# Two decode layers on one core: unread products in TensorE's gaps, seven down chunks straight to the output rows

## The chip, the cores and the metric

The kernel runs on one core of one Trainium2 chip. The metric is the time of one execution in device microseconds (us); before the change it is 1339.48 us, the median of three runs (1339.40, 1339.48 and 1342.05).

The engines are named as the profile names them: PE (TensorE, the matrix products), PEld (its weight loads), DVE (VectorE), ACT (ScalarE), POOL (GpSimd) and SP (SyncE, which here only issues DMAs).

## The reference

Two rows (batch B = 2, one token each, width D = 448) go through attention, a gated feed-forward stage, the same attention again and the same feed-forward stage again. The same weights and the same caches are read in both rounds.

```python
def _A_ref(x, k_cache, v_cache, wq, wo):           # H = 16 heads, Dh = 256, Sk = 4096 cached keys
    q = (x @ wq) ...                                # (B, H, 1, Dh)
    scores = jnp.einsum("bhqd,bhkd->bhqk", q, k_cache) * (Dh ** -0.5)
    p = _softmax(scores, axis=-1)
    o = jnp.einsum("bhqk,bhkd->bhqd", p, v_cache)
    return o ... @ wo

def _B_ref(x, W_gate, W_up, W_down):                # F = 1792
    gate = jnp.einsum("bsd,df->bsf", x, W_gate)
    up = jnp.einsum("bsd,df->bsf", x, W_up)
    h = gate * (gate > 0) * up
    return jnp.einsum("bsf,fd->bsd", h, W_down)

x = x + _A_ref(_layernorm(x), ...)
x = x + _B_ref(_layernorm(x), ...)
x = x + _A_ref(_layernorm(x), ...)
x = x + _B_ref(_layernorm(x), ...)
```

Everything is float32. The caches are 2 x 134 MB, and each of the two attention rounds (a "pass" below) reads them once, except for some chunks that stay in the core between the passes.

## The kernel before

**Tiling.** A unit u is one pair of head and batch row; a pass has 32 units (u = 0 to 31). The 4096 keys of a unit lie 32 to a partition, so a unit's keys are four chunks of 128 x 2048 numbers (1 MB), and its values four more. All loads go into one buffer, `arena`, of 27 slots of 1 MB. `pump` (L109) issues the next load on SP as soon as a slot for it has been released in the program's order; the instruction on SP then waits until the slot's last reader is done. Chunks of keys (k), chunks of values (v), the projections of a head (h: wq and wo, 896 KB), seven loads of gate and up weights (w_in, 896 KB each) and four loads of down weights (w_out, 896 or 672 KB) all pass through it in one fixed order. The last twelve k and v chunks of a pass are loaded one by one, then come the seven w_in and the four w_out. 22 slots with k, v and h of the last units of the first pass are kept, so that the second pass, which runs the units backwards, finds them in place.

**Attention.** Every step of the loop (L443 on) mixes three units: `score` of unit u on DVE and ACT (products L344, sums L349 and L346; the kept chunks at the start of the second pass take the form L338), the softmax of u, `weigh` of unit u - 1 on PE (L385), and the end of unit u - 2: `out_add` (DVE L399), `out_turn` (PE L407), `out_keep` (DVE L416) and `project` (PE L426, every second unit). `weigh` of a chunk is four products, each of two columns of probabilities with 512 numbers a row; they go to the output rows 0, 32, 64 and 96 of one half of `po_all`, one product to each strip of 32 rows. Units 30 and 31 have no more scores behind them: the last `weigh` (unit 31, chunk 3), `out_copy` (ACT L396), `out_add`, `out_turn`, `out_keep` and `project` follow each other, and `absorb` (ACT L226, PE L228, L216, L218, DVE L236) takes the pass's result into the turned row `xs`.

**Feed-forward.** `proj` (PE L477) makes the gate from w_in 0 to 3 and, after `add_rows` (L241) and the variance (L252), the up part from w_in 3 to 6: 16 products each, four at a time in four strips. DVE L500 multiplies, PE L504 and L506 turn the result, DVE L510 and ACT L515 copy it to `hT` and `tails`, and the down products (PE L528) run over 14 chunks k of 128 hidden numbers, chunk k in strip k % 4 of `pd`. After the first pass `absorb(pd, ...)` takes `pd` up; at the end of the kernel ACT L537 copies `pd` to `row`, one product (L241) adds it to `y`, the two output rows 96 and 97 of `acc`, DVE L552 copies `y`, and SP L553 stores it.

**Start of a pass.** `first_query` (L318) makes the queries of units 0 and 1 on PE (L271, L279), copies them with ACT L325 and takes the root of the variance (ACT L253). `nsr` and `sr` are written by DVE L448 and L447 after the first chunk's score; ACT L365 is the first exponential of the pass.

The lines L119, L226 and so on are those of the profile of the kernel before.

Of the kernel before, what the change touches and what calls it, by code (L numbers as in the profile page):

```python
# [8 lines left out]
F32 = mybir.dt.float32  # L9
AF = mybir.ActivationFunctionType  # L10
# [4 lines left out]
B, D, H, S, DH, F = 2, 448, 16, 4096, 256, 1792  # L15
P = 128
DC = 5
FULL, TAIL = 3, 64
# [47 lines left out]
def two_layers(  # L66
# [10 lines left out]
    nc = tc.nc  # L77
# [16 lines left out]
    pending = []  # L94
# [14 lines left out]
    def pump():  # L109
        while pending:  # L110
            (kind, name, c), n = pending[0]
            last = at_of.get((kind, name, c - 1)) if kind in "kv" else None
            at = units.take(n, kind, last)
            if at is None:
                return
            pending.pop(0)
            src = source((kind, name, c), n)
            dst = arena[:, at * UNIT : at * UNIT + src.shape[1]]
            nc.sync.dma_start(dst, src)  # L119
            for k in range(n):  # L120
                at_of[kind, name, c + k] = at + k

# [4 lines left out]
    def release(*key):  # L127
        units.free.add(at_of.pop(key))
        pump()
# [79 lines left out]
    acc = ps_a.tile([P, D], F32, name="acc")  # L209
    nc.vector.memset(acc, 0.0)  # L210
    y = acc[SUMS : SUMS + B]

    def turned(out, rows, rhs, **flags):

# [7 lines left out]
    def absorb(rows, n, rhs, nrhs):  # L222


        sums = work.tile([P, 1], F32, name="sums")
        nc.scalar.activation(row[:n, :D], rows, AF.Copy, accum_out=sums[:n])  # L226
        minus = ps_s.tile([P, B], F32, name="small")
        nc.tensor.matmul(minus, sums[:n].to_broadcast([n, P]), nrhs[:n], start=True, stop=True)  # L228
        pt = ps_s.tile([P, DC, B], F32, name="small")
        turned(pt, row[:n], rhs[:n], start=True, stop=True)  # L230
        less = work.tile([P, B], F32, name="less")
        nc.vector.tensor_copy(less, minus)
        for part in (less[:, None, :].to_broadcast([P, DC, B]), pt):
            for p, c in spans:
                x_c = xr[p, c]
                nc.vector.tensor_add(x_c, x_c, part[p, c, :, None].to_broadcast(x_c.shape))  # L236
        nc.vector.tensor_copy(xs[:, :, 32:], xs[:, :, 31:32])

    def add_rows(n, rhs, start=False, stop=False):

        nc.tensor.matmul(y, rhs[:n], row[:n, :D], start=start, stop=stop)  # L241

    def squares():
        sq = work.tile([P, FULL + 1, B], F32, name="sq")
        nc.vector.tensor_mul(sq, xT[:, : FULL + 1], xT[:, : FULL + 1])
        total = work.tile([P, B], F32, name="total")
        nc.vector.reduce_sum(total, sq.rearrange("p c b -> p b c"), axis=AX.X)
        return total

    def deviation(total):  # L250
        var = ps_s.tile([P, B], F32, name="small")
        nc.tensor.matmul(var, ones.to_broadcast([P, P]), total, start=True, stop=True)  # L252
        nc.scalar.activation(rstd, var, AF.Sqrt, bias=eps_t, scale=1.0 / D)  # L253
# [4 lines left out]
    def attention(order, after, begun):  # L258
# [58 lines left out]

        def first_query():  # L318

            total = squares()  # L320
            pq = ps_q.tile([P, B, DH], F32, name="pq")
            w = get("h", order[0][0], 0)
            for u, at in ((0, HEAD), (1, 0)):
                query_of(u, pq)
                nc.scalar.activation(w[:, at : at + DH], q_of[u], AF.Copy)  # L325
                q_of[u] = w[:, at : at + DH]
                if u == 0:
                    deviation(total)

        def score(u, c):  # L330
            kt = get("k", order[u], c).rearrange("p (t n) -> p t n", t=CT)
# [45 lines left out]
        def weigh(u, c):  # L377


            vt = get("v", order[u], c)  # L380
            if c == 0:
                po_of[u] = po_all[:, u % 2]
            for t in range(CT // 2):
                n = c * CT + 2 * t
                nc.tensor.matmul(  # L385
                    po_of[u][32 * t : 32 * t + 2, :],
                    p_of[u][:, n : n + 2],
                    vt[:, 2 * t * DH : (2 * t + 2) * DH],
                    start=(c == 0),
                    stop=(c == NC - 1),  # L390
                )
            if ("v", order[u], c) not in after:
                release("v", order[u], c)

        def out_copy(u):
            nc.scalar.activation(row[:, :DH], po_of[u][:, :DH], AF.Copy, scale=r_of[u][:, 0:1])  # L396
# [21 lines left out]
        def project(u):  # L418
            h = order[u][0]
            if u % 2 == 0:  # L420
                return
            wo = get("h", h, 0)[:, FULL * DH + P :]
            for c in range(2):
                n = u - 1 + c
                at = 32 * (n % 3)
                nc.tensor.matmul(  # L426
                    acc[at : at + B], oT_of[h][:, c, :], wo[:, c * D : (c + 1) * D],
                    start=(n < 3), stop=(n >= n_u - 3),
                )
            if ("h", h, 0) not in after:  # L430
                release("h", h, 0)

# [32 lines left out]
    def ffn(last):  # L465


        absorb(acc[:SUMS], SUMS, lead, nlead)
        total = squares()

        def proj(parts):

            p = ps_f.tile([P, D], F32, name="pf")
            for n, (part, c, done) in enumerate(parts):
                w = get("in", "", part)
                for j in range(4):
                    nc.tensor.matmul(  # L477
                        p[32 * j : 32 * j + 32, :],
                        xs[:, c, :32],
                        w[:, j * D : (j + 1) * D],  # L480
                        start=(n == 0),
                        stop=(n == 3),
                    )
                if done:
                    release("in", "", part)
            return p

        pg = proj([(0, 0, True), (1, 1, True), (2, 2, True), (3, 3, False)])  # L490
        add_rows(SUMS, lead)
        deviation(total)
        inverse()
        scaled = work.tile([P, B], F32, name="scaled")
        nc.vector.tensor_mul(scaled, sel, rstd)
        nc.vector.tensor_mul(scaled, scaled, rstd)
        hid = row[:, :D]
        nc.scalar.activation(hid, pg, AF.Relu)
        pu = proj([(3, 4, True), (4, 0, True), (5, 1, True), (6, 2, True)])
        nc.vector.tensor_mul(hid, pu, hid)  # L500

        ph = ps_f.tile([P, 4, P], F32, name="pf")
        for m in range(FULL):
            nc.tensor.transpose(ph[:, m, :], hid[:, m * P : (m + 1) * P], ident)  # L504
        for half in (0, TAIL):
            nc.tensor.matmul(  # L506
                ph[half : half + TAIL, FULL, :], hid[:, FULL * P :], ident, start=True, stop=True
            )
        hT = row[:, : FULL * P].rearrange("p (m r) -> p m r", m=FULL)
        nc.vector.tensor_copy(hT, ph[:, :FULL])  # L510

        tails = row[:, FULL * P : FULL * P + 64].rearrange("p (m r) -> p m r", m=2)
        for k, half in enumerate((slice(0, TAIL), slice(TAIL, P))):
            pairs = ph[half, FULL, :].rearrange("p (m k r) -> p k m r", m=2, k=2)
            nc.scalar.activation(tails[half], pairs[:, k], AF.Copy)  # L515

        stat = [hT[:, m, 32 * j : 32 * j + 32] for j in range(4) for m in range(FULL)]
        stat += [tails[:, m, :] for m in range(2)]
        if not last:
            nscaled = work.tile([P, B], F32, name="nscaled")  # L520
            nc.vector.tensor_scalar_mul(nscaled, scaled, -1.0 / D)
        pd = ps_f.tile([P, D], F32, name="pf")
        for j in range(4):
            w = get("out", "", j)
            first_k = (14 * j + 2) // 4
            for k in range(first_k, (14 * j + 16) // 4):
                g4 = k % 4
                nc.tensor.matmul(  # L528
                    pd[32 * g4 : 32 * g4 + 32, :],
                    stat[k],  # L530
                    w[:, (k - first_k) * D : (k - first_k + 1) * D],
                    start=(k < 4),
                    stop=(k >= 10),
                )
            release("out", "", j)
        if last:
            nc.scalar.activation(row[:, :D], pd, AF.Copy)  # L537
            add_rows(P, scaled, stop=True)
        else:
            absorb(pd, P, scaled, nscaled)  # L540
        return scaled

# [5 lines left out]
    scaled = ffn(False)  # L548
    attention(second, set(), lambda: add_rows(P, scaled))
    ffn(True)  # L550
    found = row[SUMS : SUMS + B, :D]
    nc.vector.tensor_copy(found, y)  # L552
    nc.sync.dma_start(out.rearrange("b s d -> (b s) d"), found)  # L553


# [49 lines left out]
```

## Time and profile before

| | |
|---|---|
| median of three runs | 1339.48 us |
| the profiled execution: its own time | 1341.89 us |
| its span, first to last instruction | 1340.1 us |
| outside the span | 1.8 us |
| mean granted TensorE clock | 0.672 |
| busy: DVE, PE, ACT, PEld, POOL | 76%, 42%, 30%, 14%, 8% |
| moved by DMA | 563.22 MB, mean 420 GB/s |

Times in the profile count from the first instruction of the span. "x32" behind a group of instructions is their number; every float32 product stands as two records on PE, so 16 products are x32. In the chain of waits a line gives the start, the length and what the time went to; a DMA in it is counted from its issue to its landing. In the table by stretches, the columns are the stretch, its length, the busy time of each engine with the number of instructions, the granted PE clock (1.00 is full, 0.50 half), the busy share of the DMA engines and GB/s.

### The profile page before, as it was taken

How to read it: one execution, taken by the hardware profiler on the slowest of the kernel's cores; microseconds unless marked ns; L12 is line 12 of the kernel's file. 1: busy time of each engine (PE TensorE's matmuls, PEld its weight loads, DVE VectorE, ACT ScalarE, POOL GpSimd, SP SyncE). 2: the span in 40 equal slices, each digit the busy share in tenths (PEclk: the TensorE clock that was granted, in tenths of full speed). 3: DMA queues.
4: the chain of work that ended last, by engine and by line, in shares of the span. 5: the costliest groups of instructions: out<-in, count | busy, mean ns of one | idle time of the engine just before them, and what ended most of it. 6: DMA issues, size and time to landing. Idle time of an engine off the chain costs nothing.

```text
span 1340.1 us, 10126 instructions
## 1 busy us (share of the span) xinstructions
PE 560.5 (42%) x3046; PEld 188.2 (14%) x3046; DVE 1012.3 (76%) x1180; ACT 407.1 (30%) x1730; POOL 107.1 (8%) x192
## 2 busy tenths in 40 slices
PE   3433424434244342343574444434344342443447
PEld 2111101111011110112131111111011110111112
DVE  4997876877868768677629999988778678777781
ACT  2433333333333333330012333333333333332331
POOL 0210000000000000000001111110000000000010
PEclk9667667665666676766776666675666666766668
DMA  9999999999999999999989999999999999999997
GB/s 400 431 434 429 432 425 434 431 433 428 427 433 431 433 428 430 428 436 423 419 329 365 382 423 435 433 431 430 427 434 432 427 431 433 427 432 431 434 415 298
DMA packets 29150, 563.22 MB, mean 420 GB/s; under 512 B 3236, under 2 KB 3240, under 8 KB 10024
## 3 DMA queue, kind: packets, MB, share of 16 engines
q1 hardware_dynamic: 29092, 562.58, 98.5%
q8 instruction: 24, 0.39, 0.1%
q14 instruction: 30, 0.25, 0.0%
q10 hardware_dynamic: 4, 0.00, 0.0%
HBM read 562.56 MB, written 0.00 MB: 420 GB/s over the span
## 4 chain that ended last, share of the span: by engine, by line
DMA 59%; DVE 29%; PE 8%; ACT 2%; issue 2%; POOL 0%; DVEq 0%; SPq 0%; POOLq 0%; ACTq 0%
DMA arena<-in_k_cache_dram 56%; DVE arena L344 16%; DVE scores L349 10%; DMA arena<-in_v_cache_dram 3%; PE pq L300 2%; DVE arena L338 2%; PE acc L426 2%; PE pf L477 1%; ACT arena L346 1%; DVE row L399 1%; DMA arena<-in_w_out_dram 1%; PE pq L304 1%; PE pq L271 0%; PE small L216 0%; PE pf L528 0%
## 5 line engine op out<-in xcount | busy, mean ns | idle before, releaser
L344 DVE TENSOR_TENSOR arena<-arena 128x2048 f32<-128x2048 f32 x236 | 539.3, 2285 | 152.6 <-DMA arena<-in_k_cache_dram 147.4
L346 ACT ACTIVATE arena<-arena 128x256 f32<-128x256 f32 x708 | 286.0, 405 | 539.8 <-DVE arena L344 539.8
L349 DVE TENSOR_REDUCE scores<-arena 128x5 f32<-128x1280 f32 x236 | 350.6, 1486 | 8.2
L385 PE MATMUL po<-arena,probs 128*2 128x512 f32 x2048 | 302.9, 739 | 128.9 <-DMA arena<-in_v_cache_dram 116.5
L407 PE MATMUL small<-ones,row 128*128 128x1 f32 x256 | 61.9, 346 | 414.5 <-DVE row L399 414.5
L426 PE MATMUL acc<-arena,oT 128*2 128x448 f32 x128 | 52.8, 924 | 195.0 <-DVE oT L416 195.0
L346 ACT ACTIVATION_READ_ACCUMULATOR arena<-arena 128x1 f32 x708 | 132.4, 187 | 0.0
L407 PEld LDWEIGHTS small<-ones,row 128*128 128x128 f32 x256 | 56.4, 307 | 476.6 <-DVE row L399 476.6
L385 PEld LDWEIGHTS po<-arena,probs 128*2 128x2 f32 x2048 | 55.0, 96 | 324.7 <-issue 304.1
L357 POOL PARTITION_ALL_REDUCE top<-mx x64 | 49.4, 771 | 594.4 <-DVE mx L355 594.4
L300 PE MATMUL pq<-arena,xs 128*33 128x256 f32 x174 | 74.2, 593 | 11.7 <-DMA arena<-in_w_head_dram 11.7
L316 POOL PARTITION_BROADCAST arena<-arena x58 | 30.0, 586 | 527.6 <-ACT arena L312 500.4
L355 DVE TENSOR_REDUCE mx<-scores 128x1 f32<-128x32 f32 x64 | 11.9, 186 | 69.5 <-ACT arena L346 66.0
L362 ACT ACTIVATE nm<-top,nsr 128x1 f32<-128x1 f32 x64 | 18.8, 294 | 142.5 <-POOL top L357 142.5
L312 ACT ACTIVATE arena<-pq 33x256 f32<-33x256 f32 x29 | 10.9, 376 | 140.8 <-PE pq L304 140.8
L399 DVE SCALAR_TENSOR_TENSOR row<-po,ri,row 128x256 f32<-128x256 f32 x64 | 30.5, 477 | 17.5 <-ACT row L396 17.4
L396 ACT ACTIVATE row<-po,ri 128x256 f32<-128x256 f32 x64 | 29.6, 462 | 31.8 <-PE po L385 31.8
L300 PEld LDWEIGHTS pq<-arena,xs 128*33 128x33 f32 x174 | 25.3, 163 | 80.7 <-issue 79.1
L338 DVE SCALAR_TENSOR_TENSOR junk<-arena,pq 128x256 f32<-128x256 f32 x64 | 26.9, 420 | 8.0 <-DMA arena<-in_k_cache_dram 6.0
L369 POOL PARTITION_ALL_REDUCE total<-rs x64 | 27.0, 422 | 64.3 <-ACT probs L365 64.3
L426 PEld LDWEIGHTS acc<-arena,oT 128*2 128x2 f32 x128 | 3.0, 82 | 197.7 <-DVE oT L416 197.7
L365 ACT ACTIVATE probs<-scores,nm,sr 128x32 f32<-128x32 f32 x64 | 26.4, 413 | 2.1
(94 smaller groups left out, 260.9 us busy)
## 6 DMA issues: line engine op xcount, KB each, us to landing
arena<-in_k_cache_dram SPq DMA_DIRECT2D x57, 4096.0 KB, 44.7
arena<-in_v_cache_dram SPq DMA_DIRECT2D x57, 4096.0 KB, 52.8
arena<-in_w_head_dram SPq DMA_DIRECT2D x31, 896.0 KB, 39.4
arena<-in_v_cache_dram SPq DMA_DIRECT2D x19, 1024.0 KB, 20.5
arena<-in_k_cache_dram SPq DMA_DIRECT2D x16, 1024.0 KB, 25.6
arena<-in_w_in_dram SPq DMA_DIRECT2D x14, 896.0 KB, 18.4
arena<-in_w_out_dram SPq DMA_DIRECT2D x4, 896.0 KB, 16.8
arena<-in_w_out_dram SPq DMA_DIRECT2D x4, 672.0 KB, 9.2
```

Source lines behind the costliest of these rows:

```text
L300: nc.tensor.matmul(q, xs[:, c, :], w[:, c * DH : (c + 1) * DH], start=(c == 0), stop=False)
L316: nc.gpsimd.partition_broadcast(q_of[v], found[32 * b : 32 * b + 1], channels=P)
L338: nc.vector.scalar_tensor_tensor(junk if kept else kt[:, t, :], kt[:, t, :], 1.0, q_of[u], op0=ALU.mult, op1=ALU.mult, accum_out=found[:, ...
L344: nc.vector.tensor_mul(kt, kt, q_of[u][:, None, :].to_broadcast([P, CT, DH]))
L346: nc.scalar.activation(kt[:, t, :], kt[:, t, :], AF.Copy, accum_out=found[:, t : t + 1])
L349: nc.vector.reduce_sum(found[:, BY_ACT:], kt[:, BY_ACT:, :], axis=AX.X)
L357: nc.gpsimd.partition_all_reduce(mx_of[u], mx, P, RED.max)
L385: nc.tensor.matmul(po_of[u][32 * t : 32 * t + 2, :], p_of[u][:, n : n + 2], vt[:, 2 * t * DH : (2 * t + 2) * DH], start=(c == 0), stop=(c ...
L396: nc.scalar.activation(row[:, :DH], po_of[u][:, :DH], AF.Copy, scale=r_of[u][:, 0:1])
L399: nc.vector.scalar_tensor_tensor(row[:, :DH], po_of.pop(u)[:, DH:], r_of[u][:, 1:2], row[:, :DH], op0=ALU.mult, op1=ALU.add,)
L407: nc.tensor.matmul(pT_of[u][:, c : c + 1], row[:, c * P : (c + 1) * P], ones, start=True, stop=True,)
L426: nc.tensor.matmul(acc[at : at + B], oT_of[h][:, c, :], wo[:, c * D : (c + 1) * D], start=(n < 3), stop=(n >= n_u - 3),)
```

## The change

Six edits:

- `busy(n, half)` is new: it multiplies two columns of the identity with n x 128 columns of the identity, at most 512 in one product, into output rows 0 and 1 of one half of `po_all`. Nothing reads the result. It is called after each chunk that `weigh` does for the last two units of a pass (n = 8, two products of 512), after the last `project` (n = 5, a product of 512 and one of 128) and between `absorb` and the gate products (n = 2, one of 256).
- `first_query` ends with an exponential of `eps_t` into `nsr`, which is written again by DVE later.
- In the last feed-forward stage the first seven down chunks go to `pd` as before; then `pd` is copied and added to `y`, and the chunks 7 to 13 are multiplied straight into `y`, with two columns each: `near` and `near_tails`, the columns of `hT` and `tails` that belong to the two rows, times 1/std squared.
- The last load of the kernel (w_out 3, three chunks) is issued as two DMAs: two chunks, then one.
- `y` is copied in two halves, one by DVE and one by ACT.
- Three small DVE products make `square`, `near` and `near_tails`.

```diff
+            parts = [0, src.shape[1]]
+            if not pending:
+                parts[1:1] = [src.shape[1] - D]
+            for i, j in zip(parts, parts[1:]):
+                nc.sync.dma_start(dst[:, i:j], src[:, i:j])
...
+    def busy(n, half):
+        for k in range(0, n, 4):
+            m = min(4, n - k)
+            nc.tensor.matmul(
+                po_all[:B, half, : m * P], ident[:, :B],
+                ident[:, None, :].to_broadcast([P, m, P]), start=True, stop=True,
+            )
...
+            nc.scalar.activation(nsr[:, :1], eps_t, AF.Exp)     # end of first_query
...
+            if u >= n_u - 2:                                    # end of weigh
+                busy(8, (u + 1) % 2)
...
+            if u == n_u - 1:                                    # in project, before the release
+                busy(5, 0)
...
         absorb(acc[:SUMS], SUMS, lead, nlead)
+        busy(2, 0)
         total = squares()
...
+        n_pd = 7 if last else 14
...
+                if k < n_pd:
+                    nc.tensor.matmul(
+                        pd[32 * g4 : 32 * g4 + 32, :], stat[k], w_k,
+                        start=(k < 4), stop=(k >= n_pd - 4),
+                    )
+                else:
+                    nc.tensor.matmul(y, close[k], w_k, start=False, stop=(k == 13))
+                if last and k == n_pd - 1:
+                    nc.scalar.activation(row[:, :D], pd, AF.Copy)
+                    add_rows(P, scaled)
...
-    nc.vector.tensor_copy(found, y)
+    nc.vector.tensor_copy(found[:, : D // 2], y[:, : D // 2])
+    nc.scalar.activation(found[:, D // 2 :], y[:, D // 2 :], AF.Copy)
```

In the rows that follow, each is a line of the code, the operation, output and inputs by their names in the program, the shape of what is written, and how often it stands there in a row; the line numbers of the changed kernel differ from those of the kernel before.

**PE at the end of the second pass**, from the last `weigh` of unit 30 to the gate products. Before (`po<-arena,probs` is `weigh`, `small<-ones,row` is `out_turn`, `acc<-arena,oT` is `project`):

```order
L385 MATMUL po<-arena,probs 2x512 x16
L407 MATMUL small<-ones,row 128x1 x2
L426 MATMUL acc<-arena,oT 2x448 x2
L228 MATMUL small<-nlead,sums 128x2
L216 MATMUL small<-lead,row 128x2 x3
L218 MATMUL small<-lead,row 64x2 x2
L477 MATMUL pf<-arena,xs 32x448 x16
```

After, from the last chunk of unit 31 on (`po<-ident` is `busy`):

```order
L401 MATMUL po<-arena,probs 2x512 x4
L222 MATMUL po<-ident 2x512 x2
L425 MATMUL small<-ones,row 128x1 x2
L444 MATMUL acc<-arena,oT 2x448 x2
L222 MATMUL po<-ident 2x512
L222 MATMUL po<-ident 2x128
L242 MATMUL small<-nlead,sums 128x2
L230 MATMUL small<-lead,row 128x2 x3
L232 MATMUL small<-lead,row 64x2 x2
L222 MATMUL po<-ident 2x256
L498 MATMUL pf<-arena,xs 32x448 x16
```

The first two rows of the second list stand there eight times, once for each chunk of units 30 and 31, with the `out_turn` of unit 30 between the fourth and the fifth. The end of the first pass reads the same. So 16 products of 512 columns, and behind `project` 896 columns more, stand in PE's queue at each of the two ends.

**PE at the end of the kernel**, behind the turning of the hidden row. Before:

```order
L504 MATMUL pf<-ident,row 128x128 x3
L506 MATMUL pf<-ident,row 64x128 x2
L528 MATMUL pf<-arena,row 32x448 x14
L241 MATMUL acc<-row,scaled 2x448
L591 UNCONDITIONAL_BRANCH
```

After:

```order
L525 MATMUL pf<-ident,row 128x128 x3
L527 MATMUL pf<-ident,row 64x128 x2
L568 MATMUL pf<-arena,row 32x448 x7
L255 MATMUL acc<-row,scaled 2x448
L573 MATMUL acc<-arena,near 2x448 x5
L573 MATMUL acc<-arena,near_tails 2x448 x2
L631 UNCONDITIONAL_BRANCH
```

The product with `scaled`, which needs ACT's copy of `pd`, has moved ahead of seven of the chunks, and those seven all write the rows 96 and 97 of `acc`.

**ACT at the start of the second pass**, from the take-up of the first feed-forward result to the first exponential. Before:

```order
L226 ACTIVATE row,sums<-pf 128x448
L325 ACTIVATE arena<-pq 128x256
L253 ACTIVATE rstd<-small,eps_t 128x2
L325 ACTIVATE arena<-pq 128x256
L312 ACTIVATE arena<-pq 33x256
L362 ACTIVATE nm<-top,nsr 128x1
L365 ACT_TABLE_LOAD
L365 ACTIVATE probs,rs<-scores,nm,sr 128x32
```

After:

```order
L240 ACTIVATE row,sums<-pf 128x448
L340 ACTIVATE arena<-pq 128x256
L267 ACTIVATE rstd<-small,eps_t 128x2
L340 ACTIVATE arena<-pq 128x256
L344 ACT_TABLE_LOAD
L344 ACTIVATE nsr<-eps_t 128x1
L326 ACTIVATE arena<-pq 33x256
L378 ACTIVATE nm<-top,nsr 128x1
L381 ACTIVATE probs,rs<-scores,nm,sr 128x32
```

The table load has moved from the first softmax to `first_query`, and a write of `nsr` now stands ahead of DVE's.

More of the change, by code (lines that the diff above doesn't have):

```diff
@@ L118, in pump @@
             dst = arena[:, at * UNIT : at * UNIT + src.shape[1]]
-            nc.sync.dma_start(dst, src)
+            parts = [0, src.shape[1]]
[3 more added lines that the diff above has]
+                nc.sync.dma_start(dst[:, i:j], src[:, i:j])
             for k in range(n):
@@ L521, in ffn @@
             nc.vector.tensor_scalar_mul(nscaled, scaled, -1.0 / D)
+        else:
+            square = work.tile([P, B], F32, name="square")
+            nc.vector.tensor_mul(square, rstd, rstd)
+            near = work.tile([P, FULL, 4, B], F32, name="near")
+            nc.vector.tensor_mul(
+                near, hT.rearrange("p m (j b r) -> p m j b r", j=4, b=B)[..., 0],
+                square[:, None, None, :].to_broadcast([P, FULL, 4, B]),
+            )
+            near_tails = work.tile([P, 2, B], F32, name="near_tails")
+            nc.vector.tensor_mul(
+                near_tails, tails.rearrange("p m (b r) -> p m b r", b=B)[..., 0],
+                square[:, None, :].to_broadcast([P, 2, B]),
+            )
+            close = [near[:, m, j, :] for j in range(4) for m in range(FULL)]
+            close += [near_tails[:, m, :] for m in range(2)]
         pd = ps_f.tile([P, D], F32, name="pf")
+        n_pd = 7 if last else 14
         for j in range(4):
@@ L527, in ffn @@
                 g4 = k % 4
[L528 to L534, printed above, removed]
+                w_k = w[:, (k - first_k) * D : (k - first_k + 1) * D]
+                if k < n_pd:
+                    nc.tensor.matmul(
+                        pd[32 * g4 : 32 * g4 + 32, :], stat[k], w_k,
+                        start=(k < 4), stop=(k >= n_pd - 4),
+                    )
+                else:
+                    nc.tensor.matmul(y, close[k], w_k, start=False, stop=(k == 13))
+                if last and k == n_pd - 1:
+                    nc.scalar.activation(row[:, :D], pd, AF.Copy)
+                    add_rows(P, scaled)
             release("out", "", j)
[L536 to L539, printed above, removed]
+        if not last:
             absorb(pd, P, scaled, nscaled)
```

## The prediction

> **What bounds the kernel now.** I read the table by stretches first, for the DMA column, then the chain of waits at the two places where a pass ends, then PE's timeline there. Four stretches (columns: stretch, length, busy of PE, PEld, DVE, ACT and POOL, PE clock, DMA share, GB/s):
>
> ```profile
> 671.00:678.00 7.00, 5.87 (x32) 3.00 (x32) 1.64 (x10) 1.91 (x3) 0.00 (x0) 0.50 0.24 100
> 678.00:700.00 22.00, 16.09 (x111) 6.83 (x104) 3.38 (x16) 1.76 (x6) 0.00 (x0) 0.89 0.99 388
> 700.00:740.00 40.00, 18.52 (x95) 6.37 (x94) 38.50 (x147) 9.18 (x35) 4.90 (x6) 0.71 0.90 353
> 760.00:1329.00 569.00, 242.31 (x1334) 77.19 (x1330) 444.59 (x383) 186.85 (x807) 50.76 (x84) 0.66 1.00 429
> ```
>
> From 760 us on the DMA engines are full (429 GB/s) to the end of the stream. Between the passes they starve: 100 GB/s in 671 to 678, 353 in 700 to 740. So two things count: the middle, where all that makes the next loads late is lost for good, because the stream behind it has no slack, and the tail behind the stream. Elsewhere PE can be slow for nothing.
>
> The chain in the middle:
>
> ```profile
> 675.29 5.60 PE pf L477 x32
> ...
> 684.40 9.20 DMA arena<-in_w_out_dram
> ...
> 701.09 2.85 DVE arena L338 x16
> ```
>
> The gate products (PE, half clock) free the slots of w_in 0, 1 and 2, into which w_in 5, 6 and the first w_out are loaded; the last w_out lands at 693.60, and DVE begins the second pass at 701.09. DVE runs at 38.50 of 40 us behind that, and its scores free the slots for the next loads, so its start sets when the stream is full again.
>
> The chain at the end, and the weight load that waits for the last w_out:
>
> ```profile
> 1319.35 6.13 PE pf L477 x32
> ...
> 1326.54 3.19 PE pf L477 x32
> ...
> 1335.58 0.55 ACT row L537
> ...
> 1336.18 0.93 PE acc L241 x2
> ...
> 1337.13 0.63 DVE row L552
> ```
> ```profile
> 1334.51 0.15 PEld L528 LDWEIGHTS pf<-arena,row 128*32 128x32 f32 x6 [0.78 <-DMA arena<-in_w_out_dram]
> ```
>
> PE has its other down products done just before that load lands: at the end PE and the stream arrive together, and whatever makes PE later makes the kernel longer.
>
> **The price of an unread product.** PE rows of 703 us at full clock: one product of 448 columns, and three of 256 into the same 33 rows (then two of 128). Behind them the rows of the two ends:
>
> ```profile
> 703.04 0.92 PE L241 MATMUL acc<-row,scaled 128*2 128x448 f32 x2
> 703.89 1.48 PE L300 MATMUL pq<-arena,xs 128*33 128x256 f32 x6
> ```
> ```profile
> 1307.48 0.61 PE L407 MATMUL small<-ones,row 128*128 128x1 f32 x4 [1.11 <-DVE row L399]
> 1308.02 2.76 PE L385 MATMUL po<-arena,probs 128*2 128x512 f32 x24
> 1311.67 1.04 PE L385 MATMUL po<-arena,probs 128*2 128x512 f32 x8 [0.90 <-DMA arena<-in_v_cache_dram]
> 1313.83 0.60 PE L407 MATMUL small<-ones,row 128*128 128x1 f32 x4 [1.11 <-DVE row L399]
> 1314.68 1.35 PE L426 MATMUL acc<-arena,oT 128*2 128x448 f32 x4 [0.25 <-DVE oT L416]
> ...
> 1332.08 3.38 PE L528 MATMUL pf<-arena,row 128*32 128x448 f32 x28 [0.66 <-DVE row L510]
> ```
>
> Twelve `weigh` products in three rounds of four strips take 2.76 us, one round 1.04: a further round costs 0.86, that is 0.86 for 512 columns when four strips run side by side. The unread products all write rows 0 and 1, one strip. No row has a string of them. Bounds: 0.86 / 4 = 0.215 each if products of one strip ran side by side as those of four do, 0.99 if one after the other (three of 256, 768 columns, take 1.48). I take **0.86**, since L300's three share their rows and take nearly three times 0.43. A 448-column product in a string is 0.75 by the same rate. The Trainium skill ("TensorE: Matmul & The Clock Gate", Part 3, on packing small matmuls) says that small products run side by side when each has its own strip of the array; by it one strip gains nothing and the sum stays, while at 0.215 it would end near 1333. Rows and page agree on four strips, and no row here shows two-column products packed in one.
>
> **End of the second pass.** `busy(8)` is two products, 1.7 us at full clock; seven calls (14 products, 12.0 us) stand ahead of the last `weigh`. Queued behind them on PE are the next `weigh`, `out_turn` and `project`. What they can hide in is PE's waiting: 1.11 before `out_turn` of unit 30 and 0.90 for the last v chunk; some 0.2 of run-out between rounds goes too. 12.0 - 2.2 = **+9.8** for the last `weigh`. The v chunks have landed by then, so no DMA hides it. From there to the gate products: the eighth call +0.6 (1.7 against the gap of 1.11); `project` at full clock -0.35; 640 columns (1.07) against ACT's copy (0.7) +0.4; `absorb`'s ten records -0.9 by these rows, 2.18 us at half clock (first) and 1.28 at full (second, the middle's other absorb); 256 columns (0.43) fit the 0.41 gap. Together -0.3.
>
> ```profile
> 1316.76 0.59 PE L228 MATMUL small<-nlead,sums 96*128 96x2 f32 x2 [0.72 <-ACT row L226]
> ...
> 1318.56 0.38 PE L218 MATMUL small<-lead,row 96*64 96x2 f32 x4
> 1319.35 6.13 PE L477 MATMUL pf<-arena,xs 128*32 128x448 f32 x32 [0.41 <-issue]
> ```
> ```profile
> 695.39 0.38 PE L228 MATMUL small<-nscaled,sums 128*128 128x2 f32 x2 [0.80 <-ACT row L226]
> ...
> 696.38 0.28 PE L218 MATMUL small<-scaled,row 128*64 128x2 f32 x4
> ```
>
> What the change buys is the gate at full clock: 6.13 becomes 3.2 like the up part, **-2.9**. The clock rows that say so:
>
> ```profile
> 652.86:656.27 3.41, 2.93 (x16) 1.03 (x19) 3.19 (x17) 0.00 (x0) 0.00 (x0) 0.50 1.02 423
> 1297.97:1301.38 3.41, 2.08 (x12) 0.76 (x16) 3.38 (x5) 1.03 (x6) 0.00 (x0) 0.50 1.01 420
> 1301.38:1304.80 3.42, 3.42 (x20) 1.09 (x16) 2.06 (x3) 1.94 (x9) 0.35 (x1) 0.50 1.02 419
> 1311.62:1315.04 3.42, 2.00 (x14) 0.72 (x16) 0.64 (x2) 0.47 (x1) 0.00 (x0) 1.00 1.03 428
> 1315.04:1325.28 10.24, 9.11 (x48) 3.82 (x45) 1.64 (x10) 1.91 (x3) 0.00 (x0) 0.50 1.01 418
> ```
>
> The clock changes at edges 3.41 us apart. After a stretch with 2.93 or 3.42 us of PE work it is full, after 2.08 it stays half, after 2.00 (0.6 of it one-column products) it falls. With PE never idle it will be up from the first or second edge after 1299 and stay. The same page, Part 1, says that these windows run free of the kernel, so that the moment varies; by it the rise could come up to one window earlier or later in each pass, 1.7 us of full-clock work either way, and the middle of the sum is the same.
>
> The down stage then starts +6.6 late (9.8 - 0.3 - 2.9), at 1338.7, long after the last w_out. It took 5.68 us (1332.08 to 1337.76). Now: seven chunks in two rounds 1.7; ACT's copy of `pd` 0.65 with its hand-overs, for which PE waits with all else queued behind it; `add_rows` 0.75; seven products in one strip 7 x 0.75 = 5.25 and 0.17 to run out; half a copy 0.4 instead of 0.63. Together 8.9, **+3.3**. `near` and its kin (DVE, 0.16 us each by their like) lie beside the first rounds; the split load lands before PE asks, worth nothing. If that cover went, PE arriving early, the split would save one or two products. End: 9.8 - 0.3 - 2.9 + 3.3 = **+9.9**.
>
> **The middle.** The same 12.0 us meet more waiting:
>
> ```profile
> 660.24 0.61 PE L407 MATMUL small<-ones,row 128*128 128x1 f32 x4 [1.11 <-DVE row L399]
> ...
> 663.78 1.04 PE L385 MATMUL po<-arena,probs 128*2 128x512 f32 x8 [1.10 <-DMA arena<-in_v_cache_dram]
> 666.26 1.70 PE L385 MATMUL po<-arena,probs 128*2 128x512 f32 x8 [1.44 <-DMA arena<-in_v_cache_dram]
> 669.05 1.01 PE L407 MATMUL small<-ones,row 128*128 128x1 f32 x4 [1.09 <-DVE row L399]
> 670.32 1.66 PE L426 MATMUL acc<-arena,oT 128*2 128x448 f32 x4 [0.25 <-DVE oT L416]
> ```
>
> 12.0 - 3.65 - 0.35 of run-outs = +8.0; the last `weigh`, `out_turn` and `project` at full clock -0.65, -0.4 and -0.65; `absorb` -0.9; the eighth call and the 640 columns +0.9. The gate starts **+6.3** late, at 681.6. From there to the last w_out's landing it took 18.3 us before. Its six remaining loads (four of 896 KB, two of 672) are 5.05 MB, 13.0 us at 388 GB/s; the first is let go after one round of the gate, 0.95 instead of 1.7, and the next two follow 0.75 apart instead of 1.5, so the engines start together and hardly idle. I take 15.5, **-2.8** (bounds: the 2.4 that the gate itself gains, and 3.5).
>
> `nsr`: ACT's second query copy, the table load that moves, and DVE's write of `nsr`:
>
> ```profile
> 703.15 0.39 ACT L325 ACTIVATE arena<-pq 128x256 f32<-128x256 f32 x1 [1.94 <-PE pq L279]
> ...
> 714.09 1.28 ACT L365 ACT_TABLE_LOAD   x1
> ```
> ```profile
> 704.13 0.16 DVE L448 TENSOR_SCALAR nsr<-rstd 128x2 f32<-128x2 f32 x1
> ```
>
> The exponential ends at 703.45 + 1.28 + 0.3 = 705.03; DVE's write of the same tile has to wait for it, **+0.9**, with all scores queued behind. The load that goes at 714.09 held up nobody on DVE. At the kernel's start the same wait is hidden by a full buffer of keys. Middle: 6.3 - 2.8 + 0.9 = **+4.4**.
>
> **Sum.** +9.9 + 4.4 = +14.3 us. The profiled execution took 1341.89 (1340.1 of span and 1.8 around it), 2.4 above the median of the three runs; on the median the sum gives 1353.8, and I forecast **1353.5**.
>
> **Rivals.** (1) The products hide, and the hot clock is a gain. It turns on the price of one product in one strip: at 0.215 the 14 take 3 us, less than the middle's 3.65 of waiting; the middle gains about 4.5, the end 2 (last landing 1334.5, one product, half a copy): 1333. The point is near 0.5 us a product; against it speak L300 and L241. Chance 0.08, and 0.04 for a price near that point, which gives no change (within 0.2%, 2.7 us, about what a measurement can tell). (2) The change doesn't do what it says: two columns in one strip do not count as work for the clock. Then each product costs 1.7, the gate stays at 6, the seven down products take 10.5: some +22 and +11 at the end, +20 in the middle, about 1393. For it: no stretch of one strip's work is in the trace; against: narrow products in four strips raise the clock. Chance 0.04. (3) My forecast, 0.84, of its own between 1349 and 1358: one clock window (1.7) and a run-to-run 2.5 are its width.
>
> The range 1344 to 1360 holds the last and a little of a dearer or cheaper middle. Slower 0.88, same 0.04, faster 0.08.
>
> **What would show it.** PE busy without a gap from the first `weigh` of unit 30, 1.7 us between chunks; the last `weigh` some 8 us (middle) and 10 us (end) later, long after its chunk landed; the gate at 3.2 us and clock 1.00; seven pairs of records 0.75 apart into `acc`; DVE idle 0.9 us before `nsr`. I am wrong if unread products start closer than 0.8 us to each other at full clock, or if the last `weigh` still waits for a DMA.

## The result and the profile after

| | before | after |
|---|---|---|
| median | 1339.60 us (4 runs, 1339.40 to 1342.05) | 1362.11 us (4 runs, 1359.06 to 1363.64) |
| ratio, 95% interval | | 1.0161 [1.0139, 1.0183] |
| the profiled execution and its span | 1341.89, 1340.1 us | 1359.06, 1357.3 us |

The change makes the kernel 22.5 us slower. Slower was forecast, but with 1353.5 us and an upper end of 1360, so the time lies outside the range. The two profiled executions differ by 17.2 us only: the one of before took 2.3 us more than the median of its kernel, and the one of after is the fastest of its four, 3.1 us below the median.

Three lines of the page of the kernel after: the span, the unread products (L222) as a group, and ACT's `out_copy` (L414; it is L396 in the kernel before). In a group's line, busy time and mean length (ns) stand behind the first bar; behind the second stands the engine's idle time ahead of the group, and what ended most of it.

```profile
span 1357.3 us, 10287 instructions
...
L414 ACT ACTIVATE row<-po,ri 128x256 f32<-128x256 f32 x64 | 29.6, 462 | 52.1 <-PE po L222 38.0
...
L222 PE MATMUL po<-ident 128*2 128x512 f32 (+2 forms) x76 | 36.9, 609 | 0.0
```

The middle line matters. `out_copy` reads what `weigh` made, yet 38.0 of the 52.1 us that ACT idled ahead of it were ended by an unread product. In the page of before, all of its 31.8 us were ended by `weigh` (L385). The forecast had no such wait. The 38.0 us are not its price: most of that time ACT would have waited for `weigh` anyway.

Two stretches of the kernel after, in the columns of the table by stretches:

```profile
671.00:685.00 14.00, 12.67 (x68) 4.07 (x70) 2.29 (x12) 2.39 (x4) 0.00 (x0) 1.00 0.12 49
...
760.00:1335.00 575.00, 248.06 (x1328) 77.06 (x1324) 446.77 (x376) 187.70 (x812) 51.84 (x86) 0.67 1.00 429
```

The hole in the stream between the passes is now 14 us long at 49 GB/s (before: 7 us at 100), while PE is busy 12.67 of these 14 us, at full clock, and 7.47 of them are unread products. From 760 us on the stream is as full as before, 429 GB/s.

The chain of waits at the end of the second pass:

```profile
1325.08 0.86 PE po L401 x5
1325.94 1.29 PE po L222 x3
...
1327.65 0.86 PE po L401 x5
1328.51 1.73 PE po L222 x4
1330.24 0.02 issue
1330.27 0.48 ACT row L414
...
1335.88 3.10 PE pf L498 x32
...
1347.34 0.55 ACT row L575
...
1348.85 5.28 PE acc L573 x14
```

A chunk now comes every 2.57 us (1325.08, 1327.65): 0.86 for `weigh` and 1.71 for two unread products. Behind the last chunk PE does 1.73 us of unread products first, and only then does ACT begin its `out_copy`. The gate (L498) takes 3.10 us at full clock instead of 6.13 at half. The seven down products into `y` (L573) take 5.28 us, one after the other. No DMA is left in this chain: the last v chunk landed at 1317.4, and the last `weigh` began some 9 us later (1326.64).

The middle: the chain from the gate to the end of `first_query`.

```profile
684.24 3.10 PE pf L498 x32
...
690.88 10.14 DMA arena<-in_w_out_dram
...
709.37 1.28 ACT L344
710.67 0.21 ACT nsr L344
710.90 0.17 DVE nsr L468
```

The last w_out lands at 701.03 instead of 693.60, and DVE's write of `nsr` (L468) is now in the chain behind ACT's table load and exponential.

### The profile page after: what moved, and what is told of

Its sections match the earlier page's. It is cut to its first block, busy times and chain, and to the rows that moved or that the text cites. A ratio compares the mean times of both kernels' runs of the same rounds, so it can differ in the third digit from the quotient of the medians.

```text
span 1357.3 us, 10287 instructions
## 1 busy us (share of the span) xinstructions
PE 583.2 (43%) x3122; PEld 189.5 (14%) x3122; DVE 1012.7 (75%) x1183; ACT 407.8 (30%) x1733; POOL 106.8 (8%) x192
## 4 chain that ended last, share of the span: by engine, by line
DMA 53%; DVE 32%; PE 11%; ACT 2%; issue 2%; DVEq 0%; POOL 0%; SPq 0%; POOLq 0%; ACTq 0%
DMA arena<-in_k_cache_dram 52%; DVE arena L360 16%; DVE scores L365 11%; PE pq L314 2%; PE po L222 2%; PE acc L444 2%; DVE junk L354 2%; DVE arena L354 1%; PE po L401 1%; ACT arena L362 1%; DVE row L417 1%; PE pf L498 1%; DMA arena<-in_w_out_dram 1%; PE pq L285 1%; PE pq L318 1%
## 5 line engine op out<-in xcount | busy, mean ns | idle before, releaser
L401 PE MATMUL po<-arena,probs 128*2 128x512 f32 x2048 | 315.1, 738 | 122.3 <-DMA arena<-in_v_cache_dram 112.6
L417 DVE SCALAR_TENSOR_TENSOR row<-po,ri,row 128x256 f32<-128x256 f32 x64 | 30.5, 477 | 39.5 <-ACT row L414 39.4
L414 ACT ACTIVATE row<-po,ri 128x256 f32<-128x256 f32 x64 | 29.6, 462 | 52.1 <-PE po L222 38.0
L222 PE MATMUL po<-ident 128*2 128x512 f32 (+2 forms) x76 | 36.9, 609 | 0.0
L385 POOL PARTITION_ALL_REDUCE total<-rs x64 | 24.6, 385 | 61.7 <-ACT probs L381 61.7
```

Of the source, the lines that this page charges most:

```text
L222: nc.tensor.matmul(po_all[:B, half, : m * P], ident[:, :B], ident[:, None, :].to_broadcast([P, m, P]), start=True, stop=True,)
L401: nc.tensor.matmul(po_of[u][32 * t : 32 * t + 2, :], p_of[u][:, n : n + 2], vt[:, 2 * t * DH : (2 * t + 2) * DH], start=(c == 0), stop=(c ...
L417: nc.vector.scalar_tensor_tensor(row[:, :DH], po_of.pop(u)[:, DH:], r_of[u][:, 1:2], row[:, :DH], op0=ALU.mult, op1=ALU.add,)
```

## The experiments

Each was timed against the kernel before on the same chip, and each ratio is against that kernel. The first four ran on one chip (the kernel before took 1340.07 us there), the next four on another (1340.58), the last two on a third (1340.77), so a difference between experiments of two chips can be off by some 0.7 us for that alone. A diff is against the changed kernel where the text doesn't say otherwise, and `...` marks what is left out of it.

**The changed kernel again** (no edit).

> The changed kernel again, for a second profile. Theory A (unread products in line ahead of the last weigh, out_copy of units 30 and 31 kept waiting by the products behind its own weigh, the write of nsr, the serial down products): 1359 to 1364 us, ACT's out_copy again starting within 0.1 us of the end of a product of busy. Rival B (the time above the forecast comes from where the clock's windows happen to fall): a run nearer 1363 shows a gate or a weigh at half clock that the first profile has at full, and the same out_copy waits cost nothing.

1361.41 us (4 runs), ratio 1.0162 [1.0147, 1.0177]. This run is called the control below. The time holds. In this execution, too, all four `out_copy` at the passes' ends begin within 0.1 us of the end of an unread product. Its gate between the passes started 0.9 us earlier than in the first profile, and the copy of its first query came 1.8 us later, behind products at half clock (the windows stand in the last section). So rival B has a share in the spread between executions. It does not make the 22 us: the fastest run of the changed kernel (1359.06) is 15 us above the slowest of all runs of the kernel before (1343.71), and the changed kernel's first four runs spread over 4.6.

**The products in a tile of their own.**

```diff
+    spare = []
     def busy(n, half):
...
-                po_all[:B, half, : m * P], ident[:, :B],
+                spare[0][:B, : m * P], ident[:, :B],
...
         n_u = len(order)
+        spare[:] = [ps_f.tile([P, 4 * P], F32, name="pf")]
```

> The same products write a tile of their own in place of po_all. Theory A: out_copy of units 30 and 31 then starts within 0.1 us of its own last weigh; each of the four waits of 1.7 us turns into at most 0.6, so 4.4 us less than the control (4 x 1.1), about 1357.5. Rival C (out_copy waits because it stands behind the products in PE's order, whatever they write): no change against the control, within 1 us.

1356.71 us, ratio 1.0121 [1.0106, 1.0136]: 4.7 us less than the control, as theory A has it. ACT's timeline around the end of the first pass, the changed kernel:

```profile
666.55 0.47 ACT L414 ACTIVATE row<-po,ri 128x256 f32<-128x256 f32 x1 [7.37 <-PE po L222]
678.63 0.47 ACT L414 ACTIVATE row<-po,ri 128x256 f32<-128x256 f32 x1 [11.61 <-PE po L222]
```

and with the products in their own tile (`out_copy` is L417 there, `weigh` L404):

```profile
664.71 0.47 ACT L417 ACTIVATE row<-po,ri 128x256 f32<-128x256 f32 x1 [5.51 <-PE po L404]
675.63 0.47 ACT L417 ACTIVATE row<-po,ri 128x256 f32<-128x256 f32 x1 [10.45 <-PE po L404]
```

What comes behind it on PE, in the changed kernel and then with the products in their own tile (`out_turn` is L428 there, the products L224):

```profile
676.71 1.88 PE L222 MATMUL po<-ident 128*2 128x512 f32 x4
679.68 0.61 PE L425 MATMUL small<-ones,row 128*128 128x1 f32 x4 [1.08 <-DVE row L417]
```
```profile
675.38 1.88 PE L224 MATMUL pf<-ident 128*2 128x512 f32 x4
677.19 0.61 PE L428 MATMUL small<-ones,row 128*128 128x1 f32 x4
```

In the changed kernel PE does two products for nothing and then still waits 1.08 us for DVE; with the tile of their own `out_turn` follows the products without a gap. PE's order is the same in both; what changed is whom `out_copy` waits for. So the order of PE (rival C) is not the cause. `busy` writes the half of `po_all` that `out_copy` doesn't read; the wait goes by the tile, not by the half.

**No unread product at all** (`busy` returns at once; the other edits stay).

> The change without any unread product; the exponential into nsr, the seven direct down chunks, the split load and the two half copies stay. Theory A: before + 1.0 (nsr) + 3.5 (down stage) = about 1344. Rival D (the direct chunks cost only because PE comes late; with PE on time they save the copy and the last add): before + 1.0 - 2 = about 1338.5.

1344.77 us, ratio 1.0036 [1.0022, 1.0050]. The chain of its end:

```profile
1333.50 0.55 ACT row L570
...
1335.01 5.28 PE acc L568 x14
```

With PE on time the serial down products (L568) take the same 5.28 us, and all of it stands in the chain: rival D falls. So of the 22 us about 4.7 come from the other edits, and 16.6 (1361.4 - 1344.8) from the unread products.

**The products alone**, in the kernel before.

```diff
+    def busy(n, half):
...
             if ("v", order[u], c) not in after:
                 release("v", order[u], c)
+            if u >= n_u - 2:
+                busy(8, (u + 1) % 2)
...
+            if u == n_u - 1:
+                busy(5, 0)
...
+        busy(2, 0)
         total = squares()
```

> The kernel before with the unread products alone. Theory A: the control less 4.7 (nsr 1.0, down stage 3.7), about 1357, that is 17 to 18 us above the kernel before. Rival D: the control less 1, about 1361, since the down stage costs nothing by itself.

1355.51 us, ratio 1.0120 [1.0101, 1.0138]: 15.4 us above the kernel before, and the control less 5.9. This is nearer to A (1357) than to D, which wanted 1361. The two parts alone, 15.4 and 4.7, add up to 20.1 of the control's 21.3.

**The exponential alone**, in the kernel before.

```diff
                 if u == 0:
                     deviation(total)
+            nc.scalar.activation(nsr[:, :1], eps_t, AF.Exp)
```

> The kernel before with only the exponential into nsr at the end of first_query. Theory A: DVE's write of nsr in the second pass waits some 0.9 us for it, and the stream behind takes that over: before + 0.9. Rival F (the stream makes the wait good later, as the first pass does): within 0.3 of before.

1341.44 us (12 runs) against 1340.58, ratio 1.0006 [0.9998, 1.0015]. DVE's timeline in the second pass has the wait:

```profile
702.30 0.17 DVE L449 TENSOR_SCALAR nsr<-rstd 128x2 f32<-128x2 f32 x1 [0.86 <-ACT nsr L329]
```

The wait of 0.86 us is there; whether the total takes it over stays open, since the interval holds both 0 and 0.9 us.

**Half the products**: as in the second experiment, with `busy(4, ...)` behind each chunk.

> As the kernel with the products in a tile of their own (1356.7), with one product of 512 columns per chunk in place of two. Theory A (every product ahead of the last weigh costs its 0.86 us in line): 14 x 0.43 x 2 = 12.0 less for the two of each call, that is 6.0 less at each pass's end, 1344 to 1346. Rival G (what costs is that anything stands between the chunks, not its length): less than 4 us less, above 1352.

1344.68 us, ratio 1.0040 [1.0025, 1.0055]: 12.0 us less than the second experiment. Ahead of the last `weigh` of each pass seven products of 0.86 us have gone, 14 in all, which is 12.0 us. The products cost by their length; rival G falls.

**Products only where PE waits**, in the kernel before, in a tile of their own.

```diff
+            if u == n_u - 1:
+                busy((0, 2, 4, 5)[c])
...
+            if u == n_u - 1:
+                busy(1)
...
+            if u == n_u - 1:
+                busy(3)
...
+        busy(2)
```

The four calls stand at the end of `weigh` of unit 31 for chunk c, behind its `out_turn`, in its `project` and behind `absorb`: seven products in each pass.

> The kernel before with unread products, in a tile of their own, only where PE waits at the end of a pass: 256 columns behind chunk 1 of unit 31, 512 behind chunk 2, 640 behind chunk 3, 128 behind out_turn, 384 behind project, 256 behind absorb. Theory A: no product is in the way by more than 0.2 us, the clock stays full into the gate; the middle gains 2 to 4 us, the end nothing, since PE then waits for the last w_out: 1336 to 1338. Rival H (the middle's gain is lost again while PE waits for the last w_in, as the clock falls there): 1339 to 1340.

1336.53 us (6 runs) against 1340.58, ratio 0.9967 [0.9956, 0.9978]: faster than both kernels. PE at the end of its first pass (L396 `weigh`, L218 the products, L420 `out_turn`, L495 the gate):

```profile
666.36 1.04 PE L396 MATMUL po<-arena,probs 128*2 128x512 f32 x8 [0.60 <-DMA arena<-in_v_cache_dram]
667.22 1.24 PE L218 MATMUL pf<-ident 128*2 128x512 f32 x4
668.52 0.61 PE L420 MATMUL small<-ones,row 128*128 128x1 f32 x4
...
672.69 3.38 PE L495 MATMUL pf<-arena,xs 128*32 128x448 f32 x32
```

The last `weigh` still waits for its chunk, 0.60 us, so the products ahead of it cost nothing; `out_turn` follows them without a gap; the gate starts at 672.69 instead of 675.29 and takes 3.38 us instead of 5.60. The end of the kernel gains nothing of its own: from the last but one `project` on it takes 41.7 us in this profile and 40.8 in that of before. The gate is done at full clock there, but then PE waits 0.54 and 1.23 us for the last w_in, the clock falls, and the 14 down products take 5.60 us where they took 3.38 before. PE's row of that wait and of the down products, and the windows of the clock over them:

```profile
1320.69 0.96 PE L495 MATMUL pf<-arena,xs 128*32 128x448 f32 x8 [1.23 <-DMA arena<-in_w_in_dram]
...
1324.56 5.60 PE L546 MATMUL pf<-arena,row 128*32 128x448 f32 x28 [0.66 <-DVE row L528]
```
```profile
1322.61:1329.44 6.83, 6.17 (x33) 2.08 (x34) 0.56 (x1) 0.43 (x2) 0.00 (x0) 0.50 0.28 117
```

**The same with one direct down chunk**: the last load in two parts, only chunk 13 straight into `y`, ahead of the product with `scaled`.

```diff
+        n_pd = 13 if last else 14
...
+                else:
+                    nc.scalar.activation(row[:, :D], pd, AF.Copy)
+                    nc.tensor.matmul(y, near_tail, w_k, start=False, stop=False)
```

> As e7_fit, with the last load in two parts and only the last down chunk straight into y, ahead of the product with scaled, so that it runs beside ACT's copy of pd. Theory A: with PE there before the stream, 0.5 to 0.9 us less than e7_fit. Rival I (the second, smaller DMA lands no later than the whole one did, but the first part lands hardly earlier): the same as e7_fit within 0.2.

1336.98 us (10 runs), ratio 0.9977 [0.9968, 0.9986]: no less than without it. The two intervals overlap, so a gain of 0.5 us is neither shown nor excluded. In its profile the end, from the last but one `project` on, takes 40.2 us, less than in any other profile named here, but that is one execution.

**The clock held in the wait for w_in**: the second experiment with two products of 512 columns ahead of the last group of the up part.

```diff
+        hold = {1: (4, 4)}
...
+                if c in hold and part > 3:
+                    for width in hold[c]:
+                        nc.tensor.matmul(
+                            po_all[:B, 0, : width * P], ident[:, :B],
+                            ident[:, None, :].to_broadcast([P, width, P]), start=True, stop=True,
+                        )
```

> As the kernel with the products in a tile of their own (1356.7), with two more products of 512 columns ahead of the last group of the up part, where PE waits for the last w_in in the middle (2.6 us in the changed kernel). Theory A (that wait lets the clock fall in the middle, and the down products, absorb and first_query then run at half clock in one to three windows): clock 1.00 from the gate to first_query in the middle, 2 us less from the gate's start to the second pass's first score; at the end the two products have no wait to hide in and cost 1.7; the total about the same, 1356 to 1357. Rival J (the clock there does not matter, the loads set the pace): the stretch from gate to first score as long as without them, 24 to 25 us, the total 1358.

1357.13 us, ratio 1.0121 [1.0107, 1.0135], against 1356.71 without. What it is about, in the changed kernel's first profile: PE's wait for the last w_in, and the windows of the clock behind it.

```profile
693.40 0.96 PE L498 MATMUL pf<-arena,xs 128*32 128x448 f32 x8 [2.56 <-DMA arena<-in_w_in_dram]
```
```profile
692.46:695.88 3.42, 1.67 (x15) 0.67 (x15) 0.62 (x1) 0.00 (x0) 0.00 (x0) 1.00 1.02 409
695.88:699.29 3.41, 2.76 (x18) 0.58 (x14) 0.63 (x2) 0.44 (x2) 0.00 (x0) 0.50 1.01 421
```

With the two products the clock is full from the last `weigh` into the second pass:

```profile
656.60:714.62 58.02, 46.07 (x272) 16.14 (x268) 16.51 (x88) 8.22 (x20) 1.93 (x4) 1.00 0.80 316
```

From the gate's start to the end of the first query's copy it takes 23.9 us in this execution and 24.9 without the products: 1.0 us, not 2. The gain lies behind the loads: the first query's products and copy take 2.4 us (702.42 to 704.84) instead of 4.0 (702.55 to 706.53). Up to there it takes 21.5 us instead of 20.9, so the clock makes the loads come no earlier. At the end of the kernel the two products have no wait to hide in, and the up part takes 4.9 us instead of 3.2; the total is no less. These are one execution each, and they decide between A and J only in part.

**The same idea in the faster kernel**: 256 and 640 columns in the up part of the seventh experiment's kernel.

> As e7_fit (1336.5), with 256 columns behind the second and 640 behind the third group of the up part, where PE waits 0.6 and 1.2 us for w_in in both passes. Theory A: no half clock between the last weigh and the down products' end at either pass's end; the end 1 us shorter where the clock fell there, the middle the same: 1335 to 1336.5. Rival J: the same as e7_fit or longer by the products, 1336.5 to 1338.

1336.96 us (9 runs), ratio 0.9972 [0.9962, 0.9982], the same as without. In its profile the clock stays full to the end of the kernel and the end is 0.9 us shorter than in the seventh experiment's profile (40.8 us instead of 41.7 from the last but one `project` on, what the kernel before takes), but in the middle the clock fell all the same, from 691.86 to 698.69. So A is right on the end and wrong on the middle, and the total is J's.

## Why the prediction was wrong

**The step that failed** is in the end of the second pass and again in the middle: "the eighth call +0.6 (1.7 against the gap of 1.11)", and with it the 1.11 us of waiting ahead of `out_turn` in which the products of unit 30 were to hide. Both took it that `out_copy` starts when its own `weigh` is done, and that the products run beside ACT and DVE. They run ahead of them. At each of the four places (units 30 and 31, two passes) PE does 1.73 us for nothing while `out_copy` waits, and the old gap of 1.08 to 1.11 us comes behind it in full. By the forecast's own prices that is 4 x 1.1 = 4.4 us; moving the products to a tile of their own gave back 4.7. The order of the instructions showed which products stand behind `weigh`, but not that ACT waits for them; the sum asked only who is queued behind the products on PE, not who on another engine shares their tile. Of the forecast's own signs, neither of the two for being wrong came: the products don't start closer than 0.8 us to each other, and the last `weigh` waits for no DMA. The one that failed is "PE busy without a gap".

**The second term that was mis-sized** is the -2.8 from the gate's start to the landing of the last w_out. In the first profile that took 16.9 us (684.12 to 701.03) instead of 18.3, so -1.4. In the control it was not the landing that counted but PE, which did the down products at half clock: from the gate's start to the first query's products it took 21.4 us (683.26 to 704.63), against 21.7 before (675.29 to 697.02) and 20.3 in the first profile, so -0.4. The six loads were issued closer together, as the step says, within 5.8 us instead of 7.3, but took 15.9 us from the first issue to the last landing (685.13 to 701.03), where the step left 14.6.

The other steps, against the two profiles:

- The price of an unread product, 0.86: right. A chunk with its two products takes 2.57 us, and half the products cost 12.0 us less. The products of one strip run one after the other: seven down products in one strip took 5.28 us, 0.75 each, where the four-strip down stage of before did fourteen in 3.38. The Trainium skill ("TensorE: Matmul & The Clock Gate", Part 3) says that small products run side by side when each has its own strip; the fourteen in 3.38 us agree with it.
- From the `project` of unit 29 to the gate's start, +9.5 at the end and +6.3 in the middle: it came to +10.7 (30.7 us instead of 20.1) and +8.4 (30.4 instead of 22.0). Each holds two of the four waits above, 2.2 us by the forecast's prices, so the rest was right in the middle and 1.0 too high at the end, where this error hid half of the other. With the products in a tile of their own the two are +8.2 and +6.0.
- The gate at full clock, -2.9: 3.21 us instead of 6.13, right.
- The down stage, +3.3: from its start to the store 9.4 us (1345.58 to 1355.02) instead of 5.7, +3.8. The halves of `y` account for most of the difference: they were forecast side by side and run one after the other (timeline of the kernel after).

```profile
1354.21 0.40 DVE L591 COPY row<-acc 2x224 f32<-2x224 f32 x1 [8.02 <-PE acc L573]
...
1354.65 0.35 ACT L592 ACTIVATE row<-acc 2x224 f32<-2x224 f32 x1 [6.76 <-DVE row L591]
```

- `nsr`, +0.9: the wait is there, 0.86 us, but its effect on the total was not resolved. (The forecast's sum begins at 703.45, where the row that it reads ends at 703.54; this changes nothing.)
- A stretch that the forecast left out: the first query's products and copy. They took 4.0 us before, at half clock (697.02 to 701.06), 2.4 in the first profile of the kernel after, at full (704.45 to 706.87), and again 4.0 in the control.
- Rivals: (1), cheap products that hide, was wrong in the price and wrong for products of this number and place; with the seven of each pass in the seventh experiment, fewer and fitted to the waits, the products do hide, and gain 4 us. (2) is excluded: the clock is full from 1310.27 us to the end of the kernel. In the window from 1347.81 to 1351.22 PE does nothing but products with two output rows in one strip, 3.29 us of them, and the clock stays full behind it.

The two profiles differ by 17.2 us, 2.9 more than the forecast sum of 14.3. The steps above come close to that: +1.2 and +2.1 up to the gates, +1.4 for the loads, +0.5 for the down stage, -1.6 for the first query, and -1.0 that the stream took back behind the second pass's start (by the end of `nsr` it is 6.8 us late, by the `project` of unit 29 only 5.75), together 2.6. The other 5.7 us of the whole misfit of 8.6 are not in these profiles: the forecast took the profiled execution of before to be 2.4 us above its median and put its sum on that median, that of after lies 3.1 us below its own, and the rest is rounding. Why executions of one kernel differ that much is seen only in part: the control's was 1.9 us longer than the first, and its middle, where the clock fell more often, by as much. With the wait by the tile taken out, the changed kernel's median is 1356.7 us, inside the range and 3.2 above the forecast.

## What to carry to other kernels

Work that only keeps an engine awake must fit, product by product, into waits that the timeline shows; here 12 us of it per pass, ahead of waits of 2 to 4 us, put the last `weigh` 8 to 9 us later, and the same idea cut to the gaps gained 4. Before adding a write to a tile, ask who reads any other part of that tile: here a wait between engines went by the whole tile, and a tile of its own was enough to remove it. Moving products from four strips into one took away their overlap (seven in 5.28 us, where fourteen had taken 3.38), so saving a copy that way pays only for as few of them as the copy is worth.

## What the runs showed of the hardware

The clock falls without long pauses. In the changed kernel it was half from 695.88 us on after a window of 3.42 us in which PE worked 1.67, with no pause over 2.6 us just before; in the kernel before it fell at 1315.04 after a window with 2.00 us of work and pauses of at most 1.1. The Trainium skill ("TensorE: Matmul & The Clock Gate", the table of why this matters) puts the limit at idle gaps over some 3 us; here it fell with shorter ones.

PE's busy time in a window does not decide alone. A window of the changed kernel with 1.79 us of work (689.05 to 692.46) was followed by full clock, one of the control with 2.35 us (701.12 to 704.53) by half. Over half of these 2.35 us were short products with results of 128 x 2 numbers, and 0.6 of the 2.00 above were such with 128 x 1; what else decides, no run here isolates.

Where the window edges fall differs from execution to execution, and with it which window falls: in the control two windows behind the gate were at half clock and one more in `first_query` (694.29 to 701.12 and 704.53 to 707.95), in the first profile one. Its first query's copy came 1.8 us later, though its gate had started 0.9 us earlier. This is likely a part of why the changed kernel's runs spread over 4.6 us; two profiles can't show how large a part.
